# A new account of the transposing DMA queue in a planned single-core kernel, and a new order of its work

## The chip, the cores and the metric

The kernel runs on one core of one Trainium2 chip. The metric is the device time of one execution in microseconds (us). Times before: median 148.87 us of 3 runs (148.53 to 149.22).

## The reference

Two blocks read the same normalised input and are summed with it: a linear attention with a learned feature map (Hedgehog), and a dense feed-forward block with SiLU. S = 2048 tokens, D = 448, H = 16 heads of 28, F = 1792, all in bfloat16.

```python
xn = _layernorm(x, axis=-1)
return x + _A_ref(xn, A_wqkv, A_w_phi, A_wo) + _B_ref(xn, B_w1, B_w2)

# _A_ref
q, k, v = ...                       # (x @ wqkv), 16 heads of 28
pq = einsum("bhsd,hdf->bhsf", q, w_phi); pk = einsum("bhsd,hdf->bhsf", k, w_phi)
phi_q = concatenate([softmax(pq), softmax(-pq)], -1); phi_k = the same of pk
kv = einsum("bhsf,bhsd->bhfd", phi_k, v); z = einsum("bhsf->bhf", phi_k)
num = einsum("bhqf,bhfd->bhqd", phi_q, kv)
den = einsum("bhqf,bhf->bhq", phi_q, z)[..., None] + 1e-6
return (num / den) @ wo             # heads side by side again

# _B_ref
return silu(x @ w1) @ w2
```

## The kernel before

The tokens are 16 tiles of 128 rows. Almost all matmuls use half of TensorE's rows, two at a time on the two halves (64 rows each); a pair of banks in PSUM takes a pair of blocks.

The kernel does not call the engines in the order of its text. It first records operations (`_Op`: engine, planned duration, reads, writes). `_Prog._track` finds what each depends on; `_Prog.schedule` (L216) then walks through planned time, gives each engine a list in order, and `emit_engine` writes these lists out, each with the semaphore waits it needs. On the chip each engine works through its own list in order and waits where the semaphores say. Planned times thus decide only the order within each engine.

TensorE's order is fixed beforehand: after a head (38 warming matmuls, the transposes of tiles 0 to 3 and the first three feed-forward blocks) it follows the text PLAN (L327) word by word (`strict`, L1025). The words, with a and b for the two halves of a block and @ for the banks that it opens:

- F n: block n of the first feed-forward product, 256 hidden units by 512 tokens (7 blocks for each quarter of the tokens); ACT takes SiLU of it into hT. r: the last piece of blocks 0 to 2.
- v t, k t, q t: values, key features, query features of tiles t and t+1. For k and q ACT takes exp twice, DVE sums over a head (`sums`, L786) and takes the reciprocal, POOL multiplies (`phi_k`, `phi_q`, 1.7 us a tile). f and g: the product of w_phi with wqkv that is made on the chip first.
- K t: the sums over tokens of phi_k times v, in banks 6 and 7. M: `kvm` (L832) copies them out: ACT, then kvsum and KVm on DVE; U needs KVm.
- s t: POOL's phi_q for tiles t and t+1 and their transposes.
- U p: numerator and denominator for tiles 2p and 2p+1 (`att`). It needs phqT of both tiles. DVE then divides (`normalise`: den, rden, o) into one of four o_sb slots.
- W p: the product with wo (`wo_pair`), from oT. Y p and G p: quarters of the second feed-forward product. Y leaves early: DVE copies it out (`y_ev`, L896) and so frees its banks. G shares its banks with W, and `finish_pair` then adds and sends rows out. E: two whole tiles at the end.

Four kinds of transposes go through the DMA queue of SP, all made by `dma_t` (L574), all on one list: wT (wqkv for f and g), xnT (the normalised input, tiles 4 to 15), phqT (phi_q for U; the first six tiles of the order 4, 5, 6, 7, 8, 9, 0, 1, 2, 3, 10 to 15 singly, the rest by pairs) and oT (the attention's output for W, 16 of them). The page calls them by their tiles: `wT` and `Y_sb<-in_A_wqkv_dram`, `xnT<-RA`, `phT<-RA`, `vaug<-vaug`. The order of loads and transposes up to the last wo load is pinned by a chain (L1014).

The planner's account of DMAs is in `schedule` (L296 on): `crowd` is 1 for a transpose, and `dma_free` has one time for plain DMAs and one for transposes. The lines that the change replaces:

```python
line = o.crowd
if line:
    issue_end = max(issue_end, dma_free[1] + 300.0)
dma_free[line] = max(t + min(o.dur, 1200.0), dma_free[line]) + o.xfer
o.end = dma_free[line] + o.lat
```

So a transpose is planned to take its own time on a queue that only other transposes fill. Some planned durations that matter here (in ns): a sum of a q tile 1017, its reciprocal 345, kvsum and KVm `d_dve(464)`, 643 each, y_ev 627, each less 85 for overlap.

Of the kernel before, what the change touches and what calls it, by code (L numbers as in the profile page):

```python
# [107 lines left out]
class _Op:  # L108
    __slots__ = ("id", "eng", "dur", "fn", "deps", "odeps", "table", "name", "start", "end",
                 "ticket", "sigreq", "is_dma", "xfer", "lat", "dma_sem", "dma_val", "users",  # L110
                 "out_slot", "prio", "slack", "mode", "after", "crowd")

    def __init__(self, id, eng, dur, fn, name, table=None):
        self.id = id
        self.eng = eng
        self.dur = dur
        self.fn = fn
        self.deps = set()
        self.odeps = set()
        self.table = table  # L120
        self.name = name
        self.start = None
        self.end = None
        self.ticket = None
        self.sigreq = False
        self.is_dma = False
        self.xfer = 0.0
        self.lat = 1700.0
        self.dma_sem = None
        self.dma_val = None  # L130
        self.users = []
        self.out_slot = None
        self.prio = 0
        self.slack = 0.0
        self.mode = None
        self.after = None
        self.crowd = 0


class _Prog:  # L140
# [75 lines left out]
    def schedule(self):  # L216
        ops = self.ops
        n = len(ops)
        for o in ops:
            for d in o.deps:  # L220
                ops[d].users.append(o.id)
            for d in o.odeps:
                assert ops[d].eng == o.eng, "order-only deps must be same-engine"
                ops[d].users.append(o.id)
# [15 lines left out]
        dma_free = [0.0, 0.0]  # L240
        order = {e: [] for e in ENGINES}
# [25 lines left out]
        while done < n:  # L267
# [28 lines left out]
            if o.is_dma:  # L296
                issue_end = t + o.dur
                line = o.crowd
                if line:
                    issue_end = max(issue_end, dma_free[1] + 300.0)  # L300
                dma_free[line] = max(t + min(o.dur, 1200.0), dma_free[line]) + o.xfer
                o.end = dma_free[line] + o.lat
# [19 lines left out]
MARGIN = 160.0  # L322
OVERLAP = {"dve": 85.0, "pool": 45.0}
# [3 lines left out]
PLAN = """r0 aF3@4 r2 r1 bF3 aF4@0 aF6@6 bF4 bF6 aF5@4 av2@2 bF5 bv2 av0@0 av4@6 bv0 bv4 aF10@2 aF11@4 bF10 bF11 f1@0 aF12@6 aF8@2  # L327
bF12 aF13@4 f0@0 bF13 bF8 aF18@6 ak14@0 bF18 bk14 av12@2 ak8@4 av14@6 bv12 bv14 bk8 aF9@0 aF22@2 bF9 aF14@6 bF22 av6@4
bF14 bv6 aF16@0 aF7@2 bF16 av10@6 bF7 ak6@4 bv10 bk6 av8@0 ak0@2 ak12@6 bv8 bk0 bk12 ak4@4 aF20@0 bk4 bF20 bY0@23 bY0
aF19@4 aF24@6 bF19 bF24 ak2@0 aY0 g0@5 bk2 aY0 aF17@4 aF27@6 bF17 bF27 aF21@2 aF23@0 bF21 bF23 ak10@4 K0 K12 K8 g1@0  # L330
bk10 K6 K2 K14 aq4@2 aq0@0 bq4 bq0 s4 aq6@4 K4 bq6 aY1@23 aY1 aq2@0 bY1 aq8@4 K10 M bq8 s6 bq2 bY1 aF25@6 aF26@4 bF25
aG3@01 bF26 bG3 aF15@6 aU2@45 aq10@2 bU2 s8 bF15 bG3 bq10 aU3@56 s0 aG3 bU3 bG2@47 bG2 aq12@5 s2 s10 aU4@23 bq12 bU4 s12
aW2 aG2 aq14@5 bG4@23 bq14 aG2 s14 bG4 aU1@56 bW3 bU1 aW3 bW2 aG4 aW4 aU0@56 bW4 bU0 aG4 aU5@14 bG6@07 bU5 bG5@56 aU6@23
bG5 bU6 aG5 aU7@14 aG6 bU7 aG6 aG5 aW5 aW0@23 bG6 bW0 bW5 aW6 aW1@14 bW6 aW7@235 bW1 bW7 E14 E15"""


def bass_parallel_sum__linear_kernel_hedgehog__dense_activation_silu__prompt_kernel(
# [36 lines left out]
    with es:  # L374
# [95 lines left out]
        def pe_mms(mms, name, dur=None, keys_w=(), mode=128):  # L470
            def fn(e):
                r = None
                for dst, lhsT, rhs, st, sp in mms:
                    r = e.matmul(dst, lhsT, rhs, start=st, stop=sp, skip_group_check=True)  # L474
                return r
            n = 1
            for _, cnt in mms[0][2].ap[1:]:
                n *= cnt
            return P.op("pe", dur if dur is not None else d_mm(n), fn, reads=[m[1] for m in mms] + [m[2] for m in mms],
                 writes=[m[0] for m in mms], keys_w=keys_w, name=name, mode=mode)  # L480
# [4 lines left out]
        def transposes(pairs, name):  # L485
# [5 lines left out]
            P.op("pe", 56.0 * len(pairs), fn, reads=[p[1] for p in pairs] + [ident[:]], writes=[p[0] for p in pairs], name=name, mode=128)  # L491
# [44 lines left out]
        for i in range(38):  # L536
            P.op("pe", 107.0, lambda e: e.matmul(banks[3][:, 0:128], ones_bf[:], ones_bf[:], start=True, stop=True),
                 reads=[ones_bf[:]], writes=[banks[3][:, 0:128]], name="warm", mode=128)
        P.cur_prio = 0
# [34 lines left out]
        def dma_t(dst, src, xfer, name, issue=1235.0, **kw):  # L574
            o = P.dma(lambda e: e.dma_start_transpose(out=dst, in_=src), xfer, lat=650.0, reads=[src] if kw.pop("sbuf", True) else [],  # L575
                      writes=[dst], name=name, issue=issue, **kw)
            o.crowd = 1
            o.lat += {"xnT_dma5": 700.0, "xnT_dma7": 700.0, "oT_dma": 500.0, "phqT": 500.0}.get(name, 0.0)
# [15 lines left out]
        def fold_loads():  # L594
            for i in (*range(4, NW), *range(4)):
                c = max(0, KP * i - 64)
                dma_t(wT(i), A_wqkv[:, c:c + 128], 600.0, f"wT_dma{i}", 1800.0 if i == 6 else 1310.0, sbuf=False)
# [51 lines left out]
        def ln_tile(t):  # L649
# [21 lines left out]
            if t >= XN_DMA0:  # L671
                norm(xn_sb[:, sl, 0:KF], 0, KF, 370)
                norm(xn_sb[:, sl, KF:512], D - 128, D, 250)
                if t % 2:
                    dma_t(xnT[:, t - 1:t + 1, :, :].rearrange("p i k c -> p (i k) c"),
                          xn_sb[:, sl - 1:sl + 1, :].rearrange("p i c -> p (i c)"), 2200.0 if t < 8 else 1600.0, f"xnT_dma{t}", 1350.0)
# [140 lines left out]
        def phi_q(t, pair=False):  # L817
# [8 lines left out]
            if n % 2 or not pair:  # L826
# [3 lines left out]
                      (1900.0, 2500.0)[w - 1], "phqT", (1250.0, 2000.0)[w - 1])  # L830
# [85 lines left out]
        def normalise(t, ub):  # L916
# [14 lines left out]
            dma_t(oT_sb[:, q, :, :], o_sb[:, oq, :], 650.0, "oT_dma")  # L931
# [168 lines left out]
        order = P.schedule()  # L1100
# [100 lines left out]
```

## Time and profile before

| what | value |
|---|---|
| runs | 148.53, 148.87, 149.22 us |
| the profiled execution's own time | 148.99 us |
| its span, first to last instruction | 147.7 us |
| granted clock of TensorE | 1.000 over the span |
| TensorE's idle time put down to DMAs after 100 us | 1.8 us in three waits |
| DMA transposes: of wT and Y_sb, xnT, phqT, oT | 9, 6, 11, 16 |
| phqT, oT: median from issue to landing | 4.3, 2.9 us |
| DMA transposes' issues, first and last | 7.0 and 134.8 us |

The profiled execution is 0.12 us over the median of the runs. The span is what the trace covers; 1.3 us of the execution lie around it. TensorE's matmuls are pipelined, so a block's time is best read from its first start to the first start of the next. SP is the engine that issues the loads and transposes; its rows show the issue, and the landing is told with the DMA issues. The trace's packet records add 15 instruction reads of 16 KB on queue q8, at 12.3, 20.3, 32.3, 44.0, 55.2, 67.4, 74.0, 77.3, 84.2, 95.4, 101.8, 111.3, 121.3, 127.8 and 138.3 us, and later ones of 8 KB on q14, two of them at 21.4 and 121.35 us.

### The profile page before, as it was taken

To read this page: it belongs to the slowest core of one execution; us is meant where nothing else is said; L and a number is where in the kernel's file an instruction comes from. 1 tells how busy PE (TensorE), PEld (TensorE's weight loads), DVE (VectorE), ACT (ScalarE), POOL (GpSimd) and SP (SyncE) were. 2 spreads that over 40 slices of the span, in tenths; PEclk is the share of its full clock that TensorE was granted. 3 is DMA by queue.
4 is the path that set the end of the run, shared out by engine and by line. 5 is a ranking of instruction groups with operands and counts; after the bars stand their busy time and mean duration, and the time that the engine had idled before them with its cause. 6 is when DMAs were issued, how large, how long until landed. Compare 5 with 4: busy or idle time off the path is not lost.

```text
span 147.7 us, 4511 instructions
## 1 busy us (share of the span) xinstructions
PE 141.9 (96%) x1947; PEld 90.7 (61%) x1947; DVE 90.5 (61%) x195; ACT 79.4 (54%) x96; POOL 74.9 (51%) x93
## 2 busy tenths in 40 slices
PE   7899999999999999999999999999899999879994
PEld 7694454445445544577868998855566565545763
DVE  1968997411840099666048999746965985162832
ACT  4557766579996999698678469246404000000000
POOL 8818566700394027999724989992674800000000
PEclk9999999999999999999999999999999999999999
DMA  4999999756940000000000065889494999635432
GB/s 106 340 347 249 283 145 145 135 96 178 351 134 0 0 4 0 0 0 4 0 9 0 4 119 111 92 136 152 87 170 91 212 244 188 132 73 105 130 126 62
DMA packets 44500, 17.59 MB, mean 119 GB/s; under 512 B 37040, under 2 KB 44096, under 8 KB 44480
## 3 DMA queue, kind: packets, MB, share of 16 engines
q1 hardware_dynamic: 41648, 15.10, 52.0%
q10 hardware_dynamic: 2704, 2.17, 5.2%
q8 instruction: 15, 0.25, 0.8%
q14 instruction: 5, 0.04, 0.2%
q0 software_dynamic: 128, 0.03, 0.1%
HBM read 6.57 MB, written 1.84 MB: 57 GB/s over the span
## 4 chain that ended last, share of the span: by engine, by line
PE 82%; DMA 11%; SPq 2%; DVE 2%; issue 1%
PE psum L474 82%; DMA vaug<-vaug 4%; DMA phT<-RA 4%; DMA phT<-in_B_w_dram 3%; SPq L508 1%; SPq L575 1%; DVE vaug L929 1%; DVE rden L924 0%; DVE den L922 0%; PE psum L489 0%; DVE x_sb L950 0%; SPq L1155 0%
## 5 line engine op out<-in xcount | busy, mean ns | idle before, releaser
L474 PE MATMUL psum<-xnT,phT 64*128 64x512 bf16 (+1 forms) x428 | 46.5, 350 | 0.5 <-DMA phT<-in_B_w_dram 0.3
L474 PE MATMUL psum<-w_sb,hT 64*128 64x448 bf16 (+2 forms) x434 | 46.9, 343 | 0.0
L474 PEld LDWEIGHTS psum<-w_sb,hT 64*128 64x128 bf16 (+1 forms) x434 | 27.1, 94 | 13.3 <-issue 0.2
L474 PEld LDWEIGHTS psum<-xnT,phT 64*128 64x128 bf16 (+1 forms) x428 | 24.0, 95 | 17.4 <-DMA phT<-in_B_w_dram 0.4
L494 ACT ACTIVATE hT<-psum 128x1024 bf16<-128x1024 f32 x28 | 27.5, 1023 | 12.0 <-PE psum L474 12.0
L787 DVE TENSOR_REDUCE Rec<-Ek_sb 128x32 f32<-128x896 bf16 (+1 forms) x20 | 24.4, 1252 | 13.2 <-ACT Ek_sb L494 13.2
L823 POOL TENSOR_TENSOR RA<-Ek_sb,Rec 128x896 bf16<-128x896 bf16 x16 | 27.1, 1726 | 8.0 <-DVE Rec L788 8.0
L474 PE MATMUL psum<-Wqk,xnT 64*128 64x432 bf16 x224 | 25.3, 343 | 0.2 <-issue 0.2
L494 ACT ACTIVATE Ek_sb<-psum 128x864 bf16<-128x864 f32 x24 | 20.2, 922 | 8.5 <-PE psum L474 8.5
L797 POOL TENSOR_TENSOR phT<-phT,Rec 128x896 bf16<-128x896 bf16 x8 | 13.4, 1699 | 9.6 <-DVE Rec L788 9.4
L797 POOL TENSOR_TENSOR Ek_sb<-Ek_sb,Rec 128x896 bf16<-128x896 bf16 x8 | 13.4, 1700 | 9.6 <-DVE Rec L788 9.6
L474 PEld LDWEIGHTS psum<-Wqk,xnT 64*128 64x128 bf16 x224 | 12.4, 94 | 7.8 <-issue 0.6
L494 ACT ACT_TABLE_LOAD x11 | 14.1, 1283 | 2.1 <-PE psum L474 1.1
L787 DVE TENSOR_REDUCE Rec<-phT 128x64 f32<-128x1792 bf16 x4 | 8.1, 2016 | 8.9 <-ACT phT L494 8.9
L929 DVE TENSOR_TENSOR vaug<-psum,rden 128x448 bf16<-128x448 f32 x16 | 9.4, 621 | 5.2 <-DMA vaug<-vaug 5.2
L474 PE MATMUL psum<-wo_sb,vaug 64*128 64x448 bf16 (+1 forms) x102 | 11.2, 338 | 1.4 <-DMA vaug<-vaug 1.4
L474 PE MATMUL psum<-wv,xnT 64*128 64x448 bf16 x112 | 12.2, 349 | 0.0
L652 DVE BATCH_NORM_STATS2 st<-x_sb 128x6 f32<-128x448 bf16 x16 | 9.6, 602 | 2.9 <-DMA x_sb<-in_A_x_dram 2.9
L667 DVE TENSOR_SCALAR RA<-x_sb,mv,rstd 128x384 bf16<-128x384 bf16 (+4 forms) x29 | 8.9, 346 | 1.6 <-POOL rstd L663 1.4
L950 DVE TENSOR_TENSOR x_sb<-psum,x_sb 128x448 bf16<-128x448 f32 (+1 forms) x13 | 7.1, 581 | 4.3 <-PE psum L474 4.3
L788 DVE RECIPROCAL Rec<-Rec 128x32 f32<-128x32 f32 (+1 forms) x24 | 8.7, 394 | 0.2
L474 PEld LDWEIGHTS psum<-wv,xnT 64*128 64x128 bf16 x112 | 5.5, 94 | 5.3
(60 smaller groups left out, 111.2 us busy)
## 6 DMA issues: line engine op xcount, KB each, us to landing
out_dram<-x_sb ACTq DMA_DIRECT2D x15, 112.0 KB, 3.0
w_sb<-in_B_w_dram SPq DMA_DIRECT2D x1, 1568.0 KB, 8.7
x_sb<-in_A_x_dram SPq DMA_DIRECT2D x3, 448.0 KB, 5.9
wo_sb<-in_A_wo_dram SPq DMA_DIRECT2D x2, 336.0 KB, 7.4
phT<-in_B_w_dram SPq DMA_DIRECT2D x1, 576.0 KB, 7.0
phT<-in_B_w_dram SPq DMA_DIRECT2D x2, 256.0 KB, 4.3
phT<-in_B_w_dram ACTq DMA_DIRECT2D x1, 384.0 KB, 4.6
wv<-in_A_wqkv_dram SPq DMA_DIRECT2D x1, 336.0 KB, 7.2
```

The lines of the kernel that those rows point to most:

```text
L474: r = e.matmul(dst, lhsT, rhs, start=st, stop=sp, skip_group_check=True)
L494: P.op("act", d_act(n), lambda e: e.activation(dst, src, func, scale=scale), reads=[src], writes=[dst], table=table, name=name, **keys)
L508: P.dma(lambda e: e.dma_start(out=dst, in_=src), n / 280.0, writes=[dst], name=name, eng=eng, lat=lat)
L575: o = P.dma(lambda e: e.dma_start_transpose(out=dst, in_=src), xfer, lat=650.0, reads=[src] if kw.pop("sbuf", True) else [], writes=[dst], ...
L652: P.op("dve", 590, lambda e: e.bn_stats(st6[:, t, :], xs), reads=[xs], writes=[st6[:, t, :]], name=f"bnst{t}", okeys_w=["ln"])
L667: P.op("dve", dur, lambda e: e.tensor_scalar(dst, x_sb[:, t, c0:c1], mv[:, t, 0:1], rstd[:, t:t + 1], ALU.subtract, ALU.mult), reads=[xs, ...
L787: P.op("dve", 50 + 967 * n, lambda e: e.tensor_reduce(R2, E4, AXL.X, ALU.add), reads=[E4], writes=[R2], name="Ssum")
L788: P.op("dve", 135 + 210 * n, lambda e: e.reciprocal(R2, R2), reads=[R2], writes=[R2], name="Rrec")
L797: P.op("pool", 1700, lambda e: e.tensor_tensor(E3, E3, Rk[:, :, None].broadcast_to([128, 32, DH]), ALU.mult), reads=[E3, Rk], writes=[E3], ...
L823: P.op("pool", 1700, lambda e: e.tensor_tensor(dst, Eq, Rq.rearrange("p (c j) -> p c j", c=CC)[:, :, :, None].broadcast_to([128, CC, 4, DH ...
L929: P.op("dve", 620, lambda e: e.tensor_tensor(o3, U3[:, :, 0:DH], rden[:, uq, :, None].broadcast_to([128, H, DH]), ALU.mult), reads=[U3[:, ...
L950: P.op("dve", d_dve(cs.stop - cs.start), lambda e: e.tensor_tensor(res[:, cs], ob, addend[:, cs], ALU.add), reads=[ob, addend[:, cs]], wri ...
```

## The change

Nothing is added to or taken from what the engines compute. Four things change in the planner.

1. Each TensorE operation carries `words`, two for each matmul. A new function `fetches` gives times at which instructions are read: one for every 256 words of TensorE's list, 50 words ahead, plus 400 ns, and two at DVE's 51st and 165th operation.
2. `schedule` runs twice; the second run gets these times as `stalls`. A transpose that is under way at such a time stops for 1450 ns, and an issue that ends near one ends behind it.
3. A transpose now starts 1300 ns after its issue, in the first 40 us also behind the plain loads; each output DMA pushes the transposing queue 550 ns back; and an issue waits for the third transpose before it (in the first 40 us) or for the queue (later). Transfer times and latencies of the four kinds are set anew.
4. PLAN is another text, with the same words in another order and partly other banks.

The diff, without the lines that only declare or pass on `words`:

```diff
@@ -213,9 +214,22 @@
         o.out_slot = out_slot
         return o
 
-    def schedule(self):
+    def fetches(self):
+
+        at, n, k = [], 0, 0
+        for i in self.order["pe"]:
+            n += self.ops[i].words
+            if n >= 256 * (k + 1) - FETCH_LEAD:
+                k += 1
+                at.append(self.ops[i].start + FETCH_DELAY)
+        dve = self.order["dve"]
+        return sorted(at + [self.ops[dve[n]].start + FETCH_DELAY for n in DVE_FETCHES if n < len(dve)])
+
+    def schedule(self, stalls=()):
         ops = self.ops
         n = len(ops)
+        for o in ops:
+            o.users = []
         for o in ops:
             for d in o.deps:
                 ops[d].users.append(o.id)
@@ -238,6 +252,7 @@
         eng_free = {"sp": 800.0, "act": 800.0, "pe": 0.0, "dve": 0.0, "pool": 0.0}
         act_table = [None]
         dma_free = [0.0, 0.0]
+        queued = [0.0, 0.0, 0.0]
         order = {e: [] for e in ENGINES}
         done = 0
         DELTA = 60.0
@@ -297,9 +312,27 @@
                 issue_end = t + o.dur
                 line = o.crowd
                 if line:
-                    issue_end = max(issue_end, dma_free[1] + 300.0)
-                dma_free[line] = max(t + min(o.dur, 1200.0), dma_free[line]) + o.xfer
-                o.end = dma_free[line] + o.lat
+                    for a in stalls:
+                        if a - FETCH_DELAY < issue_end < a + STALL:
+                            issue_end = a + STALL
+                    issue_end = max(issue_end, queued[-3] if t < 40000.0 else dma_free[1] + 50.0)
+                    x, rest = max(t + 1300.0, dma_free[1]), o.xfer
+                    if t < 40000.0:
+                        x = max(x, dma_free[0])
+                    for a in stalls:
+                        if a + STALL > x:
+                            if a >= x + rest:
+                                break
+                            rest -= max(0.0, a - x)
+                            x = a + STALL
+                    dma_free[1] = x + rest
+                    queued.append(x + rest)
+                    o.end = dma_free[1] + o.lat
+                else:
+                    dma_free[0] = max(t + min(o.dur, 1200.0), dma_free[0]) + o.xfer
+                    o.end = dma_free[0] + o.lat
+                    if o.out_slot is not None and dma_free[1] > t + 1100.0:
+                        dma_free[1] += 550.0
                 eng_free[o.eng] = issue_end
             else:
                 o.end = t + o.dur
@@ -320,18 +353,19 @@
 
 
 MARGIN = 160.0
+FETCH_LEAD, FETCH_DELAY, STALL, DVE_FETCHES = 50, 400.0, 1450.0, (51, 165)
 OVERLAP = {"dve": 85.0, "pool": 45.0}
 TAIL = {"act": 110.0, "dve": 85.0, "pool": 45.0}
 SIGNAL = {("act", "pe"): 60.0, ("act", "dve"): 40.0, ("dve", "pe"): 100.0, ("dve", "sp"): 30.0, ("dve", "dve"): 34.0,
           ("pool", "pe"): 100.0}
-PLAN = """r0 aF3@4 r2 r1 bF3 aF4@0 aF6@6 bF4 bF6 aF5@4 av2@2 bF5 bv2 av0@0 av4@6 bv0 bv4 aF10@2 aF11@4 bF10 bF11 f1@0 aF12@6 aF8@2
-bF12 aF13@4 f0@0 bF13 bF8 aF18@6 ak14@0 bF18 bk14 av12@2 ak8@4 av14@6 bv12 bv14 bk8 aF9@0 aF22@2 bF9 aF14@6 bF22 av6@4
-bF14 bv6 aF16@0 aF7@2 bF16 av10@6 bF7 ak6@4 bv10 bk6 av8@0 ak0@2 ak12@6 bv8 bk0 bk12 ak4@4 aF20@0 bk4 bF20 bY0@23 bY0
-aF19@4 aF24@6 bF19 bF24 ak2@0 aY0 g0@5 bk2 aY0 aF17@4 aF27@6 bF17 bF27 aF21@2 aF23@0 bF21 bF23 ak10@4 K0 K12 K8 g1@0
-bk10 K6 K2 K14 aq4@2 aq0@0 bq4 bq0 s4 aq6@4 K4 bq6 aY1@23 aY1 aq2@0 bY1 aq8@4 K10 M bq8 s6 bq2 bY1 aF25@6 aF26@4 bF25
-aG3@01 bF26 bG3 aF15@6 aU2@45 aq10@2 bU2 s8 bF15 bG3 bq10 aU3@56 s0 aG3 bU3 bG2@47 bG2 aq12@5 s2 s10 aU4@23 bq12 bU4 s12
-aW2 aG2 aq14@5 bG4@23 bq14 aG2 s14 bG4 aU1@56 bW3 bU1 aW3 bW2 aG4 aW4 aU0@56 bW4 bU0 aG4 aU5@14 bG6@07 bU5 bG5@56 aU6@23
-bG5 bU6 aG5 aU7@14 aG6 bU7 aG6 aG5 aW5 aW0@23 bG6 bW0 bW5 aW6 aW1@14 bW6 aW7@235 bW1 bW7 E14 E15"""
+PLAN = """r0 aF3@4 r2 r1 bF3 aF6@0 aF4@6 bF6 bF4 aF5@4 av2@2 av0@0 bv2 bF5 av4@6 bv0 bv4 aF10@2 aF9@0 bF10 f0@6 bF9 aF12@4 aF7@2
+aF11@0 f1@6 bF11 bF7 bF12 aF25@0 ak2@6 bF25 bk2 av8@4 av12@2 bv8 ak0@0 bv12 bk0 av10@6 aF22@4 bv10 aF17@2 bF22 av14@6
+aF14@0 bF17 bv14 aF18@4 bF14 aF27@6 ak4@2 bF27 bF18 bk4 av6@6 ak6@0 ak8@4 bv6 bk8 bk6 ak12@2 aF8@6 bk12 bF8 aY0@45
+aF21@0 aY0 aF23@2 bF21 bF23 ak14@6 bY0 g0@1 bk14 bY0 aF13@0 aF19@2 bF13 aF20@4 bF19 aF24@6 bF20 bF24 ak10@0 g1@3 bk10 K0
+K6 K4 aq4@2 K12 aq8@4 bq4 K8 K2 s4 aq0@0 bq8 aq6@2 K14 bq0 bq6 bY1@45 K10 M aY1 aq2@2 aF26@0 s6 bq2 bY1 bF26 aG3@23 aY1
+aU2@67 s8 aF15@0 bU2 s0 bF15 aF16@4 bG3 bF16 aU4@01 aq12@6 bU4 bq12 aU3@45 bG3 bU3 s2 aG3 aq10@0 aq14@6 bq10 s10 aW2@45
+bq14 aG2 aU0@01 bG2 aG4@67 bU0 bW4 bG2 bW2 s12 bG4 aG2 s14 aW3 aG4 aU1@01 bW3 aW4 bU1 bG4 bG5@23 aU5@50 aG6@41 aU6@67
+bU5 aG5 bG6 aU7@05 bU6 bG5 bG6 aG5 bU7 aG6 aW0@67 bW5 bW0 aW5 aW6 aW1@05 bW6 bW7@672 bW1 aW7 E14 E15"""
 
 
 def bass_parallel_sum__linear_kernel_hedgehog__dense_activation_silu__prompt_kernel(
@@ -571,11 +609,11 @@
             load(wo_sb[:, i, :, :], A_wo[64 * i:64 * i + KF, :].rearrange("(k p) d -> p k d", p=128), f"wo{i}")
             load(wor_sb[64 * i:64 * i + 64, :], A_wo[KF * (1 - i):KF * (1 - i) + 64, :], f"wor{i}")
 
-        def dma_t(dst, src, xfer, name, issue=1235.0, **kw):
-            o = P.dma(lambda e: e.dma_start_transpose(out=dst, in_=src), xfer, lat=650.0, reads=[src] if kw.pop("sbuf", True) else [],
+        def dma_t(dst, src, xfer, name, issue=1235.0, lat=550.0, **kw):
+            o = P.dma(lambda e: e.dma_start_transpose(out=dst, in_=src), xfer, reads=[src] if kw.pop("sbuf", True) else [],
                       writes=[dst], name=name, issue=issue, **kw)
             o.crowd = 1
-            o.lat += {"xnT_dma5": 700.0, "xnT_dma7": 700.0, "oT_dma": 500.0, "phqT": 500.0}.get(name, 0.0)
+            o.lat = lat
 
 
         def fold():
@@ -594,7 +632,7 @@
         def fold_loads():
             for i in (*range(4, NW), *range(4)):
                 c = max(0, KP * i - 64)
-                dma_t(wT(i), A_wqkv[:, c:c + 128], 600.0, f"wT_dma{i}", 1800.0 if i == 6 else 1310.0, sbuf=False)
+                dma_t(wT(i), A_wqkv[:, c:c + 128], 450.0, f"wT_dma{i}", 1750.0 if i == 6 else 1290.0, lat=950.0, sbuf=False)
 
         PW = 2 * DH
         LO_HI = (slice(0, 64), slice(64, 128))
@@ -673,7 +711,7 @@
                 norm(xn_sb[:, sl, KF:512], D - 128, D, 250)
                 if t % 2:
                     dma_t(xnT[:, t - 1:t + 1, :, :].rearrange("p i k c -> p (i k) c"),
-                          xn_sb[:, sl - 1:sl + 1, :].rearrange("p i c -> p (i c)"), 2200.0 if t < 8 else 1600.0, f"xnT_dma{t}", 1350.0)
+                          xn_sb[:, sl - 1:sl + 1, :].rearrange("p i c -> p (i c)"), 950.0, f"xnT_dma{t}", 1330.0, lat=850.0)
                 return
 
             def turn_over(k0, k1, b, tag):
@@ -827,7 +865,7 @@
                 n0, sp0 = (slot(t) - 1, sp - 1) if pair else (slot(t), sp)
                 w = slot(t) - n0 + 1
                 dma_t(phT[:, n0:n0 + w, :, :].rearrange("p t c j -> p (t c) j"), phq[:, sp0:sp0 + w, :, :].rearrange("p n c j -> p (n c j)"),
-                      (1900.0, 2500.0)[w - 1], "phqT", (1250.0, 2000.0)[w - 1])
+                      (1250.0, 2450.0)[w - 1], "phqT", (1250.0, 2000.0)[w - 1])
 
         def kvm():
             lo, hi = (banks[KVB - i][0:KP, 0:2 * DA * CC] for i in range(2))
@@ -928,7 +966,7 @@
             o3 = o_sb[:, oq, off:off + D].rearrange("p (h d) -> p h d", d=DH)
             P.op("dve", 620, lambda e: e.tensor_tensor(o3, U3[:, :, 0:DH], rden[:, uq, :, None].broadcast_to([128, H, DH]), ALU.mult),
                  reads=[U3[:, :, 0:DH], rden[:, uq, :]], writes=[o3], name="o")
-            dma_t(oT_sb[:, q, :, :], o_sb[:, oq, :], 650.0, "oT_dma")
+            dma_t(oT_sb[:, q, :, :], o_sb[:, oq, :], 620.0, "oT_dma")
 
         def wo_pair(p, turned, bs, last):
             both = []
@@ -1097,7 +1135,8 @@
                 t = int(arg)
                 ffn2_full(t, bank_of[t // 2][t % 2])
             strict(n0)
-        order = P.schedule()
+        P.schedule()
+        order = P.schedule(P.fetches())
         ops = P.ops
 
         def needs_sem(d, o):
```

## The prediction

> **What bounds the kernel now.** First the page's head and share of busy time, then the chain of waits in order of time, then TensorE's own waits.
>
> ```profile
> span 147.7 us, 4511 instructions
> ...
> PE 141.9 (96%) x1947; PEld 90.7 (61%) x1947; DVE 90.5 (61%) x195; ACT 79.4 (54%) x96; POOL 74.9 (51%) x93
> ...
> 101.79 3.72 DMA vaug<-vaug
> 105.51 0.35 issue
> 105.86 12.99 PE psum L474 x190
> ...
> 121.12 5.52 DMA phT<-RA
> 126.64 0.14 issue
> 126.78 1.97 PE psum L474 x46
> ...
> 129.56 2.43 DMA vaug<-vaug
> 131.99 0.14 issue
> 132.12 13.58 PE psum L474 x126
> ```
>
> TensorE sets the end, and what it loses it loses in three places, each time to a transposing DMA: at 105.86 (W2 waits for oT of tile 5), 126.78 (U7 waits for phqT of tiles 14, 15), 132.12 (W5 waits for oT of tile 11).
>
> How much is that? The trace gives each block start to start; the TensorE timeline shows how.
>
> ```profile
> 90.68 1.57 PE L474 MATMUL psum<-w_sb,hT 64*128 64x448 bf16 x14
> 92.00 1.11 PE L474 MATMUL psum<-xnT,phT 64*128 64x512 bf16 x8
> 92.87 1.57 PE L474 MATMUL psum<-w_sb,hT 64*128 64x448 bf16 x14
> 94.19 0.90 PE L474 MATMUL psum<-xnT,phT 64*128 64x512 bf16 x6
> 94.84 0.47 PE L474 MATMUL psum<-KVm,phT 64*128 64x58 bf16 x16
> 95.19 0.72 PE L474 MATMUL psum<-Wqk,xnT 64*128 64x432 bf16 x6
> ```
>
> A G word of 14 matmuls takes 92.00-90.68 = 1.32, bF 0.87, aF 0.65. Read so throughout: v 0.57+0.76, k and q 0.55+0.73, U 0.23, W 0.76+0.57, K 0.505, f 0.22, g 0.255, r 0.217, E14 2.66, E15 2.85. The words after the head (which ends at 11.40) make 25 F 37.8, 8 v 10.6, 16 k and q 20.5, 28 Y and G 37.0, 16 U 3.7, 16 W 10.6, 8 K 4.0, f, g, r 1.6, E 5.5: 131.4, so laid end to end they end at 142.8. The last matmul ends at 145.7. **Waiting is 2.9**: 0.80 at W2, 0.57 at U7, 0.93 at W5, 0.42 among the K words at 75.3 to 76.3, some 0.2 in crumbs. (Start to start; as idle time the first three read 0.64, 0.39, 0.75, because a matmul's modelled end reaches into the wait.) Nothing else can be won by an order.
>
> **Why the transposes are late.** The DMA view of 94 to 137, 40 slices of 1.075 us:
>
> ```profile
> GB/s 0 135 4 190 199 216 211 165 5 97 83 76 113 167 216 205 91 68 62 213 205 216 218 245 229 261 21 211 290 299 86 90 101 5 122 115 76 74 101 122
> ...
> q8 instruction: 5, 0.08, 0.9%
> ```
>
> Traffic drops to 4, 5, 21 and 5 GB/s in the slices at 96, 103, 122 and 129.5. Four of the five instruction reads of this stretch (packet records: 95.4, 101.8, 121.3, 127.8) lie just ahead of these. The transposes behind them land late: phqT 9 is issued at 97.93 and lands 6.1 later (median of its kind 4.3), oT 2 5.7 and oT 1 4.4 (median 2.9), so 1.5 to 2.8 each. SP issues transposes without a gap from 94.2 to 136: the queue itself is nearly full.
>
> A page of the Trainium skill speaks against the account: "Runtime: NRT & Kernel Launch", section Instruction fetch mechanics, says that instructions come in 16 KiB blocks and that crossing one is mostly hidden. 15 reads and 0.25 MB on the page agree on the size; the four slices say that for the transposes they are not hidden. By that rule alone the new order plans around waits that do not exist, and the sum would be that of the third case below.
>
> **The change part by part.** The new fields, the second pass and the new constants put no instruction on the chip: cost 0. What arrives there is an order. The PLAN holds the same words, so the 131.4 and the head stay (same chain of the early loads on SP). Where the old words stand in the trace, and the new ones laid end to end without waits: bk10 ends 73.8 / 72.4, K10 begins 85.2 / 82.4, U2 94.8 / 91.0, W2 105.9 / 102.5, U7 126.8 / 124.7, W5 132.1 / 131.4, W7 138.2 / 135.4, end 145.7 / 142.8. U now goes 2, 4, 3, 0, 1, 5, 6, 7.
>
> *Early part, to 72.* In the old trace no word between 12 and 74 waits. New tight places: F25 at 30.1 needs xnT of tiles 14, 15 (landed 28.9: cover 1.1); q6 at 78.6 needs ACT's second exp of q4: bq4 ends 76.26, +0.26 +1.70 = 78.2; K0 at 72.41 needs F24's silu, 72.2. ACT starts pairs every 0.8. Cost 0.3, bounds 0 and 0.8: the old K stretch is the nearest row (0.42 + 0.14), and the new one has fewer K words in a row.
>
> *DVE from 78 to 94.* This is the new wait I see. The old row:
>
> ```profile
> 79.84 2.08 DVE L787 TENSOR_REDUCE Rec<-Ek_sb 128x32 f32<-128x896 bf16 x2 [0.59 <-ACT Ek_sb L494]
> ...
> 87.72 1.53 DVE L837 TENSOR_TENSOR KVm<-kvsum,mask 112x464 bf16<-112x464 f32 x1
> ...
> 94.04 1.08 DVE L898 TENSOR_TENSOR Y_sb<-psum,x_sb 128x448 f32<-128x448 f32 x2
> ```
>
> DVE works from 79.84 to 95.13 without idling: five q pairs (2.46 each), kvsum and KVm 2.1, y_ev 1.1. Already in the old order q10, on the banks that y_ev frees, begins at 95.19, right behind it. The planner books KVm at 0.56, not 1.53. In the new order q4's sums can begin at 78.3 (bq4 76.26 + 0.26 + 1.70 + 0.1); the same 15.3 behind that ends y_ev at 93.6. U2 at 91.0 finds KVm at 78.3 + 4x2.46 + 2.1 = 90.3: fits by 0.7. But F16@4 at 92.95 reuses the banks of Y1@45 and must wait for y_ev: **0.7**. If y_ev goes ahead of q2's sums the wait is 0; if DVE runs 0.5 later, 1.2. I take 0.7.
>
> *Transposes of the tail.* Old: POOL hands over 4 and 5 at 84.9 and 86.5, and 8, 9 only behind the pair (0,1). New: k10's phik end at 81.5 (exps to 75.4, DVE 2.6, POOL 3.35), so phiq 4, 5, 8, 9, 6, 7 end at 83.2, 84.9, 86.6, 88.3, 90.0, 91.7. Six single transposes are thus gone before U2 has made the first oT (y_ev 93.6 + 1.3: 94.9). In the old trace 8 and 9, with their issues at 95.81 and 97.93, stood in the full stretch: 3.9 of it. SP's new list from there, with 1.27 an oT and 1.9 to 2.5 a pair (the old issue rows), all users 0.7 later for F16, and the reads where the old ones came by count of matmuls (1354, 1476, 1648, 1766: here 99.9, 109, 120.7, 127), 1.5 each: oT 4, pair (0,1), oT 5 are issued by 99.4, and oT 5 lands by 102, behind a read (W2 103.2: cover 1.2). oT 8, pair (2,3), oT 9, 6, 7 follow until 108; oT 6, 7 land by 109 (W3 114.2). Pair (12,13): POOL ends at 107.8, issue to 110, (U6 122.3). U0 is done at 109.1, its oT 0 goes at 110.3, pair (10,11) behind it, whose sums DVE ends at 107.7 and POOL at 111.2: lands by 117 (U5 120.7). Pair (14,15), POOL at 114.6, lands by 121 (U7 125.4, cover 4; in the old trace it was issued at 121.12, 2.85 after POOL had it ready). U1 is done at 118.1: oT 2, 3 to 123.5 with a read; U5 at 122.7: oT 10, 11 land by 127.5 (W5 132.1); U7 at 130.0: oT 15, bound by U7 itself, lands by 135.1 (W7 136.1, cover 1). So the three waits, 2.3 in all, go. Residue 0.2, bounds 0 and 2.3 (they stay). If a cover were gone, the next transpose would be late by the same, SP issuing in order.
>
> ACT's kinds change over as often in the new words, so its 11 table loads of 1.28 stay. Idle time of DVE, ACT or POOL that comes or goes elsewhere is worth 0: TensorE's 96% cover it. The end behind W7 (E14, E15, last DMA) is the same.
>
> **Sum**, against the profiled execution's own 148.99 (span 147.7): 148.99 - 2.9 + 0.3 + 0.7 + 0.2 = 147.3. The median of the runs shown is 148.87, 0.12 lower: about 147.2; I say 147.3. A measurement of this kernel can tell 0.5% (0.74) from no change.
>
> **Rivals.**
> 1. *As forecast*, 147.3, own range 146.7 to 148.1: chance 0.42.
> 2. *All waits go*, y_ev too: 148.99 - 2.9 + 0.1 - 0.1 = 146.1. For it: no wait from 12 to 74 in the old trace, where the planner's account also held. Against: KVm's 1.53 is not in it. 0.15.
> 3. *No net gain; the account does not meet the chip.* If the late landings come from a full queue and not from reads, or the reads come elsewhere, the old three waits return in another place: 146.1 + 1.0 + 2.3 - 0.1 = 149.3; with part of them 148.5. For it: SP's unbroken issues; reads in the old trace come after 76 to 172 matmuls, while the account has one every 128. Against: two transposes fewer in the full stretch. 0.20, around 148.8.
> 4. *Slower: reads uncovered.* Five reads fall between 92 and 136. One that strikes a transpose whose user has 1 of cover costs TensorE its 1.5 to 2.8 less that 1, and SP, which issues in order, passes it to the next ones, whose cover is then gone. One such read gives case 3; from the second on, each at a full 2.0, it is slower: 146.1 + 0.7 + 0.3 + 4.0 - 0.1 = 151.0. For it: the covers are of the size of an account's error (a read off by 25 matmuls is 2 us off). Against: in the old trace the same reads cost 2.3 with a fuller queue. 0.23.
>
> **How the numbers follow.** 147.3 is the likeliest case. The range goes from all waits gone (146.0) to one and a half uncovered reads (150.4), leaving out some 0.2. Faster (under 148.13): 0.41 of case 1 and all of 2, 0.56; within 0.5%: case 3 and the rim, 0.21; slower (over 149.61): 0.23.
>
> **What would show it.** Right: no DMA in TensorE's waits at W2, U7 and W5; U2 at about 91; TensorE idle near 93, released by y_ev on DVE, 0.5 to 1; last matmul at 143.5 to 144.5. Wrong: a wait of over 1 for a transpose behind 100 (case 3, two of them case 4), a wait between 12 and 72, or U2 later than 92.

## The result and the profile after

| | before | after |
|---|---|---|
| median, both on the same chip | 148.97 us (148.53 to 149.45, 6 runs) | 146.46 us (146.14 to 147.0, 6 runs) |
| the profiled execution's own time | 148.99 us | 146.37 us |
| last matmul ends | 145.69 us | 143.06 us |
| words laid end to end | 142.8 us | 142.8 us |

The changed kernel takes 0.9835 of the time before, 95% interval 0.9807 to 0.9863: faster by 2.5 us. Here and below a median is that of all runs, and a ratio leaves out the slow ones, those more than 1.5% above their kernel's fastest. All of it is TensorE's: from the last matmul to the end of the execution it is 3.30 us before and 3.31 after. TensorE now loses 0.26 us against its words laid end to end, where it lost 2.9.

The page of the changed kernel, head and shares:

```profile
span 145.1 us, 4509 instructions
...
PE 141.6 (98%) x1947; PEld 83.6 (58%) x1947; DVE 89.5 (62%) x195; ACT 79.4 (55%) x96; POOL 75.1 (52%) x93
...
PE 93%; DMA 3%; SPq 1%; DVE 0%; issue 0%
```

The end of its chain of waits (start, length, what), and all that TensorE waits for in it:

```profile
9.50 30.98 PE psum L508 x345
40.48 0.01 issue
40.48 102.59 PE psum L508 x1503
143.07 0.02 issue
143.10 0.39 DVE x_sb L988
```

```profile
PE psum L574 <- POOL epst L538: 1.1, 1, 1.1
PE psum L508 <- ACT xnT L531: 0.2, 1, 0.2
```

Before, the chain was cut three times behind 100 us by a DMA. After, one unbroken run of matmuls goes from 40.48 to the last one. The wait of 1.1 is that of the first warming matmul and was there before too. Idle time by the releaser shows nothing else; start to start one word behind the head is long, the second half of F22 at 39.45 (1.04 instead of 0.87: 0.18; the chain has the end of that wait at 40.48).

What the blocks that had waited find now (landings from the DMA issues, starts from TensorE's rows; the cover of a block is the time from the landing of what it needs to its start):

| block, transpose | before: landed, began | after: landed, began | cover after |
|---|---|---|---|
| W2, oT of tile 5 | 105.51, 105.86 (waited 0.80) | 98.48, 102.63 | 4.15 |
| U7, phqT of 14, 15 | 126.64, 126.78 (waited 0.57) | 123.09, 124.85 | 1.76 |
| W5, oT of tile 11 | 131.99, 132.12 (waited 0.93) | 128.21, 131.6 | 3.4 |
| W7's second half, oT of tile 15 | 137.26, 139.50 | 134.64, 135.56 | 0.92 |

One thing about the change itself can be read from the planner. With the new PLAN, the old account, the new one, and the new one without reads give the same order on all five engines. So what reaches the chip is the PLAN text alone; the account matters through which PLAN the search found.

### The profile page after: what moved, and what is told of

The parts are those of the page before. It is cut to its first block, busy times and chain, and to the rows that moved or that the text cites. A ratio compares the mean times of both kernels' runs of the same rounds, so it can differ in the third digit from the quotient of the medians.

```text
span 145.1 us, 4509 instructions
## 1 busy us (share of the span) xinstructions
PE 141.6 (98%) x1947; PEld 83.6 (58%) x1947; DVE 89.5 (62%) x195; ACT 79.4 (55%) x96; POOL 75.1 (52%) x93
## 3 DMA queue, kind: packets, MB, share of 16 engines
q10 hardware_dynamic: 2704, 2.17, 5.3%
## 4 chain that ended last, share of the span: by engine, by line
PE 93%; DMA 3%; SPq 1%; DVE 0%; issue 0%
PE psum L508 93%; DMA phT<-in_B_w_dram 3%; SPq L545 1%; PE psum L525 0%; DVE x_sb L988 0%
## 5 line engine op out<-in xcount | busy, mean ns | idle before, releaser
L508 PE MATMUL psum<-w_sb,hT 64*128 64x448 bf16 (+2 forms) x434 | 46.1, 343 | 0.0
L508 PEld LDWEIGHTS psum<-xnT,phT 64*128 64x128 bf16 (+1 forms) x428 | 22.5, 95 | 18.5 <-ACT vaug L531 0.6
L508 PEld LDWEIGHTS psum<-w_sb,hT 64*128 64x128 bf16 (+1 forms) x434 | 23.2, 94 | 17.2 <-issue 0.2
L508 PE MATMUL psum<-Wqk,xnT 64*128 64x432 bf16 x224 | 24.4, 343 | 0.0
L531 ACT ACTIVATE Ek_sb<-psum 128x864 bf16<-128x864 f32 x24 | 20.3, 915 | 5.9 <-PE psum L508 3.7
L508 PEld LDWEIGHTS psum<-Wqk,xnT 64*128 64x128 bf16 x224 | 11.2, 95 | 8.1
L508 PE MATMUL psum<-wo_sb,vaug 64*128 64x448 bf16 (+1 forms) x102 | 10.7, 338 | 0.0
```

The costliest lines, as they stand in the source:

```text
L531: P.op("act", d_act(n), lambda e: e.activation(dst, src, func, scale=scale), reads=[src], writes=[dst], table=table, name=name, **keys)
```

## The experiments

Those of one chip are compared with the kernel before on that chip. Its median is 148.68 for the account alone, the two runs with later reads and KVm by itself; 148.56 for the two with oT issued again and for the pair (14,15) moved, alone and with later reads; 148.4 for earlier reads, the two with free copies and the pair (0,1) moved.

**The account without the PLAN.** The changed planner with the old text; on the chip, pair (0,1) goes behind oT of 4 and 5, and pair (14,15) behind oT of 0, 1 and 10 to 13.

```diff
-PLAN = """(the new text)"""
+PLAN = """(the old text)"""
```

> The new account with the old PLAN. TensorE's order is the old one; on SP the account puts pair (0,1) behind oT 4 and 5, and pair (14,15) behind the six oT of tiles 0, 1, 10 to 13, which before came after it. Theory (the gain lies in the order of the words; an account is worth only the PLAN that it picks): U7 now waits until oT 12 and 13 are out (U6 done 125, issued to 129) and the pair behind them lands, at about 132 instead of 126.6; the wait at W5, 0.9, falls inside it; so 148.9 + 5.4 - 0.9 = 153.4, range 151.5 to 155. Rival (the account gives better lists whatever the PLAN): faster than before, 146.5 to 148.3.

157.28 us (156.3 to 158.13), ratio 1.0584 (1.0522 to 1.0646). The chain, and the granted clock by stretches (length, busy time of TensorE, clock, DMA share, GB/s):

```profile
128.60 4.30 DMA phT<-RA
132.90 0.14 issue
133.04 20.75 PE psum L508 x200
```

```profile
118.00:124.00 6.00, 6.00 (x121) 1.00 1.17 202
124.00:133.00 9.00, 0.92 (x10) 0.75 0.61 117
133.00:136.00 3.00, 2.96 (x31) 0.50 0.02 5
136.00:139.00 3.00, 3.00 (x34) 0.54 0.00 0
139.00:142.00 3.00, 3.00 (x36) 1.00 0.46 90
```

U7 waits 8.1 us for the pair that the new account sent late; the 0.93 at W5 is gone, as expected. Of the 3.9 over the expectation, 0.9 is that the pair lands at 132.90 and not at 132. Some 2.8 is something that nobody had on the list: behind the idle time the clock is 0.50 until about 138.8, and a G word takes 2.59 and 2.48 instead of 1.32. So the account by itself, put on the old words, harms: it moves the pair that U7 needs behind six transposes that nothing needs so soon.

**The reads moved.** To the chip, instructions are read by their count, not by the work in them: the first two reads came after 136 and 212 matmuls in the kernel before, and after 124 and 210 with fewer and wider warming ones. So ten warming matmuls do the work of 38, so that everything behind keeps its time while TensorE's reads should come 28 matmuls later (the first two came at 14.2 and 22.7 us instead of 12.3 and 20.3; of the five behind 94 in the kernel before, four came 22 to 62 matmuls later in the work, and the one of 121.3 came at 119.5, at the same point of the work). Once in the kernel before, once in the changed one.

```diff
-for i in range(38):
-    matmul(banks[3][:, 0:128], ones_bf, ones_bf)
+for r in (4,) * 9 + (2,):
+    matmul(banks[3][:, 0:128 * r], ones_bf, ones_bf repeated r times)
```

> The kernel before, its 38 warming matmuls of 128 columns replaced by 10 of the same columns in all: 28 matmuls fewer on TensorE's list, all lists else the same. Theory (an instruction read stops the transposes): the reads come 28 matmuls later in the work, near 97.0, 104.0, 113.3, 122.7 and 129.3 instead of 95.5, 101.8, 111.3, 121.3 and 127.8, and the slices of almost no traffic move with them; the waits at W2, U7 and W5 change one by one, by up to 1.5 each, either way; sum 147.5 to 150.5. Rival (the transposes are late because the queue is full, and the reads only fall there): the empty slices stay near 96, 103, 122 and 129.5, the same three waits, 148.9 within 0.3.

> The changed kernel with the same 28 matmuls fewer. Reads near 95.7, 103.9, 112.2, 121.9, 128.1 and 138.1 instead of 92.7, 101.3, 109.4, 120.3, 125.5 and 135.6. Theory (the new order has 0.9 to 4 us of cover at each word): the empty slices move, TensorE still waits for no transpose or for one of under 0.5: 146.5, range 146.1 to 147.2. Rival (the order fits because the reads fall just where the account put them): 1 to 2 us of waits return, 147.5 to 148.5.

Before with later reads: 147.67 us (147.25 to 148.7), ratio 0.996 (0.9924 to 0.9997). The changed kernel with later reads: 146.40 (146.12 to 146.82), ratio 0.9855 (0.9812 to 0.9897), that of the changed kernel. TensorE's first row of waits, and the DMA view of 94 to 137, in the kernel before with later reads:

```profile
PE psum L474 <- DMA phT<-RA: 1.1, 1, 1.1
```

```profile
GB/s 73 186 121 108 238 210 177 105 90 60 82 79 215 212 147 121 94 222 35 124 287 314 334 265 103 23 93 254 306 186 113 129 9 121 122 119 83 50 77 213
...
q8 instruction: 5, 0.08, 0.8%
```

Each slice is 1.075 us. The empty slices of the kernel before lay at 96, 103, 122 and 129.5, behind its reads at 95.4, 101.8, 121.3 and 127.8. Now the thin ones are at 113 (35 GB/s), 121 (23) and 128 (9), at or just behind the reads of 113.3, 119.5 and 128.0; those of 96.0 and 103.1 leave no empty slice. They held up transposes all the same: the phqT issued at 95.16 took 3.76 to its landing where the one ahead of it took 3.04, the oT issued at 102.08 took 3.77 where the one ahead took 2.51. The operations, their order and the queue's load are the same, and yet the waits at W2 and W5 have vanished, and the 0.42 among the K words too, while U7's has grown from 0.57 to 1.28. So a read does stop the transposes, and where it falls decides which block waits.

By the place of the reads alone the old order thus gains 0.6 (by the ratio) to 1.0 (by the medians) of the 2.5 that the change gains. The changed kernel neither gains nor loses by it: TensorE's waits in it with later reads, but for the first warming matmul's, are one row, and that lies in the head, at 7.95.

```profile
PE psum L508 <- DMA phT<-in_B_w_dram: 0.5, 1, 0.5
```

Its covers take the stops.

**The changed kernel with its reads half a distance away.** The same trick to the other side, 102 narrow warming matmuls (32 rows out, 48 columns) for 38, so that TensorE's reads should come 64 matmuls earlier.

> The changed kernel with its reads 64 matmuls earlier, half the distance of two reads, as far from where the account has them as can be: 102 narrow warming matmuls instead of 38. TensorE's reads then come at about 95.5, 103.5, 114.5, 119.8 and 129.7. Theory (the covers of 0.9 to 4.2 take one read wherever it falls, at most one is used up): 146.4 (146.2 to 147.2). Rival (the order fits only because the reads come where it was searched for them): a wait of 1 to 2 at U7 or at W6 and W7, 147.4 to 149.

147.33 us (146.94 to 147.66), ratio 0.9926 (0.9895 to 0.9957). Its chain of waits from 9.7 on:

```profile
9.73 10.70 PE psum L508 x118
20.43 0.08 issue
20.51 20.45 PE psum L508 x228
40.96 0.01 issue
40.97 102.73 PE psum L508 x1503
143.69 0.02 issue
```

The chain is again unbroken from 40.97 to the end, with reads at 99.3, 106.8, 115.1, 124.1 and 129.3: neither U7 nor W6 nor W7 waits, and the rival (a fit to the places of the reads) falls for the tail. The expected time was 0.9 too low. The profiled execution, at 147.10, shows 0.62 more to the last matmul: against the changed kernel TensorE is 0.24 behind from 8.0 on, another 0.24 from 20.5 (behind F5) and another 0.19 from 75.8 (behind K12), and nothing more from there to the end. The new warming and the part ahead of 76 pay, not the transposes behind 90. The other 0.2 of the median no profile shows.

**KVm by itself.** The forecast had F16 wait 0.7 for y_ev; the trace after shows no such wait. DVE's rows there in the changed kernel:

```profile
88.11 0.58 DVE L873 TENSOR_TENSOR kvsum<-psum,kvsum 112x464 f32<-112x464 f32 x1
88.60 1.07 DVE L825 TENSOR_REDUCE Rec<-Ek_sb 128x32 f32<-128x896 bf16 x1
89.59 0.85 DVE L875 TENSOR_TENSOR KVm<-kvsum,mask 112x464 bf16<-112x464 f32 x1
...
91.95 1.09 DVE L936 TENSOR_TENSOR Y_sb<-psum,x_sb 128x448 f32<-128x448 f32 x2
```

POOL's two operations around KVm, in the changed kernel and then in the one before:

```profile
88.24 1.70 POOL L861 TENSOR_TENSOR RA<-Ek_sb,Rec 128x896 bf16<-128x896 bf16 x1
...
89.90 2.10 POOL L861 TENSOR_TENSOR RA<-Ek_sb,Rec 128x896 bf16<-128x896 bf16 x1
```

```profile
87.06 1.70 POOL L823 TENSOR_TENSOR RA<-Ek_sb,Rec 128x896 bf16<-128x896 bf16 x1 [0.54 <-DVE Rec L788]
...
88.72 2.10 POOL L823 TENSOR_TENSOR RA<-Ek_sb,Rec 128x896 bf16<-128x896 bf16 x1
```

After, POOL's operation ends at 89.94 and KVm at 90.44; before, at 88.76 and 89.25. KVm thus ends some 0.49 behind POOL's running operation whenever it began, and the next one of POOL takes 2.10 instead of 1.70. After, a sum stands between kvsum and KVm, so KVm began only 0.35 ahead of POOL's end (0.85 in all), before 1.04 ahead (1.53). The Trainium skill, "SBUF — State Buffer", section "SBUF: two separate sides", says the same of an operation of DVE with two SBUF inputs against one of GpSimd: whoever starts first holds the shared ports for the whole instruction, the other blocks. The rows agree, to the 0.40 that POOL then loses. To see what 0.85 saved, KVm was put directly behind kvsum, ahead of the sum:

```diff
 o = P.op("dve", d_dve(464), ...)          # kvm
+kvm_op.append(o.id)
...
 o = P.op("dve", 50 + 967 * n, ...)        # Ssum
+if kvm_op:
+    o.odeps.add(kvm_op[0])
+    o.odeps -= o.deps
```

> The changed kernel with one order on DVE undone: KVm directly behind kvsum, as before, and q2's first sum behind it. Theory (KVm cannot run beside POOL's operation: it lasts until that one ends, and 0.5 more; and the wait of F16 for y_ev was real): KVm starts at 88.7, POOL's operation ends at 89.9, so KVm ends at 90.4 and lasts 1.8 instead of 0.85, POOL's next operation 2.1 instead of 1.7; y_ev ends at 94.0 instead of 93.0 and F16 starts 0.9 later: 147.4, range 147.0 to 147.8. Rival (KVm's length has another cause, or F16 does not hang on y_ev): 146.5 within 0.3.

148.23 us (147.34 to 148.85), ratio 0.9968 (0.9933 to 1.0003). The expectation was 147.4. KVm's row, F16's row and TensorE's waits in it:

```profile
88.65 1.73 DVE L880 TENSOR_TENSOR KVm<-kvsum,mask 112x464 bf16<-112x464 f32 x1
```

```profile
93.90 0.82 PE L508 MATMUL psum<-xnT,phT 64*128 64x512 bf16 x6 [0.71 <-DVE Y_sb L942]
```

```profile
PE psum L508 <- DVE Y_sb L942: 0.7, 1, 0.7
PE psum L508 <- DVE x_sb L994: 0.7, 1, 0.7
```

The first half is as expected: KVm takes 1.73, y_ev ends at 93.84 instead of 93.04, and F16 begins at 93.90 instead of 93.10. It waits 0.71 as idle time and 0.88 start to start, near the 0.7 that the forecast had booked. The second wait, 0.85 start to start at the second half of W7 (137.19), was not expected. Its releaser reads x_sb on DVE, but oT of tile 15, issued at 132.98, landed only at 137.06: reads came at 135.0 and 135.6 while it was under way. That is the cover of 0.92, the least of all, eaten by reads, a small case of the fourth rival. That the runs of 147.3 and 147.4 had only the first wait is likely; no profile shows one.

**Two transposes more in the queue.** In the changed kernel and in the one before, two more ahead of the pair (14,15). The first form issued oT of two tiles again:

```diff
 dma_t(oT_sb[:, q, :, :], o_sb[:, oq, :], ..., "oT_dma")
+if t in (0, 1):                           # (2, 3) in the kernel before
+    dma_t(oT_sb[:, q, :, :], o_sb[:, oq, :], ..., "oT_dma")
```

> The changed kernel with two transposes more in the queue: oT of tiles 0 and 1 is each issued twice, ahead of the pair (14,15). Nothing else moves. Theory (the queue, and within it the cover of each block, sets the waits): each added transpose takes SP 1.27 us, so the pair is issued 2.5 later and lands at about 125.6 instead of 123.09; U7, whose cover was 1.76, waits 0.8, and the time is 146.4 + 0.8 = 147.2 (146.6 to 148.3, by whether a read then falls on it). Rival (the queue has room and takes the two in its gaps): no wait, 146.4. Rival (the tail is covered by one read at most, so any lateness brings the old waits back): 148.7.

> The kernel before with the same two transposes more: oT of tiles 2 and 3 is each issued twice, ahead of the pair (14,15). Theory (the old order has no room left in the queue): the pair lands 2.5 later and U7's wait grows from 0.57 to about 3, while the 0.93 at W5 goes into it or stays: 148.8 + 2.0 to 2.6 = 151.1 (150.2 to 152.0). Rival (late landings came from the reads alone and the queue has gaps): 148.8 to 149.2.

151.57 us (ratio 1.0252, 1.0186 to 1.0317) and 154.93 (1.042, 1.0335 to 1.0505): far over the expectation, because the edit costs more than two transposes. The chain of the first:

```profile
117.21 5.16 DMA vaug<-vaug
122.37 0.02 issue
122.39 1.19 SPq L615
...
123.68 4.38 DMA phT<-RA
128.06 0.05 issue
```

The second copy of an oT writes where the first writes, so SP holds it until the first has landed (for tile 1 from 117.21 to 122.37), and the pair behind goes at 123.68, 7.4 later than in the changed kernel. U7 waits 3.2, and behind it the clock is down: 0.57 from 128 to 131. In the kernel before U7 waits 4.5, and the clock is 0.50 from 130 to 136. The runs say what a pair some 4 to 5 us late costs, not what a fuller queue does. So it was done again with copies that wait for nothing, from W_o into a buffer that nobody reads:

```diff
+if t in (0, 1):                           # in the kernel before: (2, 3)
+    dma_t(spare[:, t % 2, :, :], wo_sb[:, 0, :, :] as 128 x 512, ..., "spare_dma")
```

> The changed kernel with two more transposes ahead of the pair (14,15), now from a constant (W_o) into a buffer that nothing reads, so that they wait for nothing and nothing waits for them but the queue behind. Theory (in the changed order a late pair eats its cover first): the pair lands 2.5 later, at about 125.6; U7's cover of 1.76 goes and 0.8 of wait is left, too short for the clock to fall: 147.2 (146.6 to 147.9). Rival (the queue takes them in its gaps): 146.4. Rival (any lateness there becomes a wait of 3 and a slower clock, as with the copies that waited for their twins): 150 to 151.5.

> The kernel before with the same two free transposes ahead of the pair (14,15). Theory (no cover and no gap left there): U7's wait grows from 0.57 to about 3.1, at which the granted clock halves for one G word (1.3); the 0.93 at W5 goes into it: 148.6 + 2.5 + 1.3 - 0.9 = 151.5 (150.2 to 152.5). Rival (the old queue has gaps that take them): 148.6 to 149.2.

148.03 us (147.12 to 149.66; ratio 0.9979, 0.9936 to 1.0022) and 150.63 (150.09 to 151.75; ratio 1.019, 1.0088 to 1.0292). TensorE's waits behind 100 us, in the changed kernel with the two, and in the one before with them:

```profile
PE psum L509 <- DMA phT<-RA: 1.0, 1, 1.0
```

```profile
PE psum L475 <- DMA phT<-RA: 2.0, 1, 2.0
...
PE psum L475 <- DMA vaug<-vaug: 1.0, 1, 1.0
...
PE psum L475 <- issue: 0.3, 1, 0.3
```

The profiled execution of the changed kernel, at 147.49, has the one wait expected: the pair lands at 125.93, 2.84 later, and U7 waits 1.15 start to start (expected 0.8). The median is 0.8 over the expectation, and what the runs of 148 and more wait for no profile shows. In the kernel before, 0.4 at W2, 2.17 at U7 and 1.24 at W5: the wait at U7 stays under 3, the clock at 1.00, and so the time under the 151.5 expected. Set against 146.46 (on another chip) and 148.4, the two transposes cost 1.6 and 2.2. In the profiles the cover of 1.76 takes part of it in the one; the other has none.

**One transpose moved in the kernel before.** First the pair (14,15) ahead of oT of 2 and 3; then the same with the reads 28 matmuls later; then, alone, the pair (0,1) behind oT of 4 and 5.

```diff
-T11 T13 o2 o3 T15 o0 o1
+T11 T13 T15 o2 o3 o0 o1
```

```diff
-T8 T9 T1 o4 o5 o6 o7
+T8 T9 o4 o5 T1 o6 o7
```

(T: phqT, a pair by its second tile; o: oT.)

> The kernel before with one transpose moved: the pair (14,15), which POOL had ready 2.85 us before its issue, goes ahead of oT of tiles 2 and 3. Theory (the queue as a whole is late, so a better place for one transpose only hands the lateness on): U7's wait of 0.57 goes, W5 then comes 0.57 earlier to an oT of tile 11 that lands when it did, and its wait grows from 0.93 to about 1.5: no net gain, 148.8 (148.4 to 149.2). Rival (a place in the order was all that was wrong with it): 148.2 with the wait at W5 as it was.

> The same move in the kernel before with the reads 28 matmuls later, where the one wait left was 1.28 at U7. Theory: U7's wait goes; W5 then comes at about 129.3, and oT of tile 11, issued at 126.2 with a read at 128 on top, landed at 130.4: a wait of about 1.1 in its place, 147.5 (147.0 to 147.9). Rival (with the reads off the way and the pair in its place nothing is late): 146.4, the time of the changed kernel with the old order otherwise.

> The kernel before with one transpose moved: the pair (0,1), which U0 needs only at 117.6, goes behind oT of tiles 4 and 5, which W2 waits for at 105.9. Nothing else moves. Theory A (the old queue as a whole is late): W2's 0.80 goes and comes back at U7 and W5: 148.6 (148.2 to 149.0). Theory B (the wait at W2 was a bad place, and TensorE's lateness there makes all later transposes late): as in the first part of the run with the account alone, the landings behind come 1.3 earlier; the pair (14,15) lands at about 125.2, U7 no longer waits, W5 still 0.8: 147.2 (146.8 to 147.8).

The first: 149.49 us, ratio 1.0058 (1.0016 to 1.01), a little slower. The second: 148.75, ratio 1.0017 (0.9975 to 1.006), 1.1 over the same reads without the move (on another chip) and 1.2 over the theory's 147.5. The third: 148.39, ratio 1.0021 (0.9974 to 1.0067). None gains, and each rival with a gain falls in the median. The chain of the first shows the new form of the wait:

```profile
117.68 4.31 SPq L577
121.99 0.05 issue
122.05 4.46 DMA vaug<-vaug
126.50 0.03 issue
...
127.14 0.62 DVE vaug L936
127.76 0.05 issue
127.81 4.60 PE psum L474 x74
```

The pair is issued 3.4 earlier (117.68 for 121.12), holds SP for 4.31 and lands at 126.14, only 0.5 earlier. oT of tile 2 goes behind it and lands at 126.50; until then its o_sb slot is taken, DVE cannot write the next o, and U7 waits for the bank that this o would empty: 2.2 start to start, where it had waited 0.57. W5's wait is gone, and W7 has one of 0.9 for oT of tile 15, which a read at 137.1 met under way. That is worse than the theory, by a road that it did not have.

The profile of the second has the same road, and longer. It is of the longest of its ten runs (150.64): the pair is issued at 117.09 and lands at 126.01, oT of tile 2 lands at 126.61, and no other wait of TensorE behind 100 is left. The clock is at half from 128 to 131 (0.50 in the second row).

```profile
PE psum L474 <- DVE vaug L936: 2.9, 1, 2.9
```

```profile
128.00:131.00 3.00, 3.00 (x34) 1.42 (x36) 1.42 (x5) 0.00 (x0) 0.00 (x0) 0.50 0.80 60
```

So the wait came at U7, not at W5 as the theory had it. In the third the profiled execution (147.85) shows W2's wait gone and U7's grown to 0.82, W5's 0.47; in its median nothing is left of that. By its median theory A holds there, and B was 1.2 too low; the profiled execution is 0.5 under that median, and what the longer runs wait for no profile shows. None of these moves mends the old order, and in the two profiles of the pair (14,15) what U7 was to gain comes back as a longer wait.

## Why the prediction was right, point by point

*The waits.* Right. The three waits of 2.3 at W2, U7 and W5 are gone, by the mechanism named: the transposes of 4 to 9 are all issued before the first oT, the last at 92.03, and SP, which had next to no gap from 94.2 on, has some now (117.82 to 118.97, 122.69 to 123.56, 129.69 to 130.90). The two free copies test it: with two transposes put back U7 waits again, 1.15. U2 starts at 91.10, as said. The 0.42 among the K words went too; the old order loses it as well when only its reads move.

*Which transpose was late.* The forecast called the transpose issued at 97.93, which landed 6.1 later, phqT 9. It was the pair (0,1); 8 and 9 went at 94.16 and 95.81. Nothing in the sum hung on it but the "3.9 of the full stretch" (3.8 by the right rows). That it was 1.8 late holds by luck: the 4.3 that it was set against is the median over singles and pairs, and it is also what a pair takes with no read on it and no pair close ahead (4.3, issued at 107.00 and at 112.89 before). With a read on it this pair takes 6.1 after as well (97.23 to 103.33, read at 101.3).

*Early part, 0.3.* It measured 0.18, at F22, which was not among the tight places listed: the size was right, the place was not. F25, q6 and K0 did not wait.

*y_ev, 0.7.* The step that was mis-sized: 0. The sums of q4 begin at 78.43 (forecast 78.3), but y_ev ends at 93.04, not 93.6, because KVm took 0.85 and the forecast carried over the 1.53 of the old row. The page gives 1.53 as the time of an operation that was mostly waiting for POOL, and in the new order it meets POOL near an end. With KVm directly behind kvsum the wait is there (0.71 idle, 0.88 start to start). F16 starts at 93.10, right behind y_ev: there was nothing to spare. So one of the signs named failed: TensorE is not idle near 93.

*Tail, 0.2.* Under 0.1 is left. Two covers were misjudged: U7's is 1.76, not 4 (the read at 120.3 lies on its pair, issued at 116.30), and W2's is 4.15, not 1.2. W7's is 0.92, as said. With all that TensorE still loses, 0.26, the sum is 148.99 - 2.9 + 0.26 = 146.35, against 146.37 measured; that shows that the loss is all TensorE's, and no more, since the 0.26 is itself measured. So the forecast's 147.3 was 0.9 high, 0.7 of it y_ev's. The last matmul, at 143.06, is ahead of the 143.5 to 144.5 named, and 146.46 is below the first case's own 146.7 to 148.1. The outcome lies nearer to the second rival, 146.1, than to the first: all waits go, y_ev's too. The range held because it reached down to that rival.

*The rivals that did not come.* The third (a full queue, or reads elsewhere, bring the waits back) describes the kernel before in part: none of the three moves gains there, and two free copies cost 2.2, yet moving its reads alone gains 0.6 to 1.0. It does not hold for the new order, which takes reads in three different places without a wait in the tail. The fourth came in a small form only, with KVm moved: 0.85 at W7, where the cover was least. The account that it doubted is indeed of no use by itself: alone it costs 5.8%.

## What to carry to other kernels

A duration in a profile may hold a wait for another engine's port; before carrying it into a new order, look at what ran beside it and where that ends. In a queue that was almost never free, none of three moves of one transfer gained anything; six transposes taken ahead of the full stretch, with cover for the users in it, made the waits go. And judge an order by the cover of each block as well as by its waits: 0.9 to 4 us of it is what took the reads here.

## What the runs showed of the hardware that was not expected

TensorE's clock halves behind an idle time of some 3 us, and that doubles the price of a long wait's first blocks. Waits of 2.0 (twice) left it at 1.00. Behind 2.9 (the pair and the reads moved together) it was 0.50 over the next 3 us, behind 3.2 it was 0.57; behind 4.5 it was 0.50 for 6 us, behind 8.1 it was 0.50 to 0.54 for 5.5 us, 2.8 us lost. The Trainium skill, "TensorE: Matmul & The Clock Gate", section Part 1: The HAM clock gate (the "warmup" mystery), has half the clock after an idle window of about 3.4 us and as long a busy one to get back. The runs agree on the half. As for the idle time, 2.9 was already enough, and the way back took 3 to 6 us from the first matmul on.

An instruction read (16 KB on q8 or 8 KB on q14) stops the DMA transposes under way. Taken over all fourteen traces, of the oT that go out with at most 1.35 us of an earlier transpose still to land, 89 have no read between issue and landing: 85 of them take 2.4 to 2.6 us, the other four 3.5 to 3.9. With a read 1.0 to 2.1 us behind the issue, 21 take 3.8 to 5.2. A read in the last 0.2 us ahead of the landing changes nothing (2.4 to 2.6, five of them). So the price is as a rule 1.3 to 1.9 us on the transpose under way, and by SP's order on what stands behind it. It does not always show as an empty slice of the DMA view: in the kernel before slices of 4 to 21 GB/s stand behind four of its reads, with later reads slices of 9 to 35 behind three. The pair issued at 116.30 in the changed kernel, with reads at 120.3 and 120.9, took 6.8, where pairs without one took 4.3.
